# A fused attention and FFN kernel: final maxima moved to GpSimd, output tiles in halves, smaller last units split by head pair

## The chip, the cores and the metric

The kernel runs on one core of a Trainium2 chip. A core has five engines with queues of their own: TensorE (PE in the profile, its weight loads PEld), VectorE (DVE), ScalarE (ACT), GpSimd (POOL) and SyncE (SP), which here only issues DMAs. Matrix products land in PSUM, eight banks of 128 partitions x 512 fp32; everything else lives in SBUF. The metric is the device time of one execution in microseconds (us). Before the change it is 1213.11 us, the median of three runs (1212.67 to 1213.38).

## The reference

One layer with S = 2048 rows and D = 512 columns in bfloat16. `xn` is the layer norm of `x`. The result is `x + attention(xn) + ffn(xn)`:

```python
xn = _layernorm(x, axis=-1)
# attention: H = 32 heads of Dh = 16
qkv = (xn @ wqkv).reshape(B, S, 3, H, Dh).transpose(2, 0, 3, 1, 4)
q, k, v = qkv[0], qkv[1], qkv[2]
scores = jnp.einsum("bhqd,bhkd->bhqk", q, k) * (Dh ** -0.5)
p = _softmax(scores, axis=-1)
o = jnp.einsum("bhqk,bhkd->bhqd", p, v)
attn = o.transpose(0, 2, 1, 3).reshape(B, S, D) @ wo
# FFN: F = 1792
h = _silu(xn @ w1) * (xn @ w3)
out = x + attn + h @ w2
```

The softmax runs over 2048 keys for each of 32 x 2048 rows, so 134 million scores are computed, and their maximum per row is subtracted.

## The kernel before, in words

**Tiling.** Rows (queries) are cut into four chunks of 512 (`qc`), the 32 heads into eight groups of four (`g`). A pair (`qc`, `g`) is a head group; there are 32 of them, taken in order of `qc`, then `g`. Each is cut into *units* of 256 query rows; the first head group is cut 128, 128, 256 (`UNIT_HEAD`), and the last three into four units of 128 (`UNIT_TAIL`). That makes 71 units.

**First pass (p1).** For each unit the scores are computed with the queries on the partitions: one tile is 128 queries x 512 keys x two heads (a head pair), two matmuls in two row groups of PE (L878), into two PSUM banks. DVE reduces a tile to the maxima of its 128 rows for two heads (`part`, L900, 128x2 from 128x1024). There are 1024 such tiles, with two slots of two banks, so PE can write one tile while DVE reads the other. After a unit's last tile the maxima over the four key chunks are joined to `negm`, the negated row maximum (`final_max`, L941, on DVE). This instruction stands in DVE's queue behind one more tile of the next unit (`pend_fin`).

**The maximum enters the second scores as two more rows.** GpSimd splits `negm` in two bfloat16 numbers (L917 and L919, into `Z`). SP then transposes `Z` by DMA into `Zs` (L938) and copies two rows per head into the query tile `QT` (L934, two issues). For the units in `FAST_AUG` (the first two and the last four, `NFAST`) PE does this instead: the tile `QT2` projects the queries again from `xnT` (four groups of matmuls) and adds the transposed `Z` (one group for each 128 rows), and ACT copies it to `QT` (L696). For the last unit the two splitting steps are on DVE.

**Second pass (p2).** The scores are computed again with the keys on the partitions and the maximum already subtracted (L1014, one tile of 128 x 512, four of 256-column or 128-column matmuls by unit size), and ACT takes the exponential into `PT` (L1027, 2048 of them). Four PSUM banks serve p2 and all other products. A unit's tiles come for its four heads in turn.

**PV and the division.** `PT` times `V` with a column of ones gives 16 numbers and the sum for each head (`tile_PV`). ACT copies it to `U` (L1091); three small DMAs and GpSimd bring the reciprocal of the sums to all partitions (L1112, L1116, L1121, L1125), and GpSimd multiplies into `onorm` (L1136). For the units in `FAST_PV` (the last three, `NFPV`) PE also forms the sums over a block of ones, and DVE takes the reciprocal (L1081) and the product (L1083) from PSUM.

**FFN and output.** `ffn_pair` computes 128 columns of the hidden layer for 512 rows (two PE tiles, three copies on ACT, three steps on GpSimd, L720, L722, L724). An output tile of 128 rows (`tile_OUT`, 12 of them) is one accumulation over `x` (by the identity), 14 FFN groups and eight attention groups, copied by ACT (L802) and stored. The last four output tiles are in two passes: `tile_OUTA` holds `x` and the FFN part and is copied to SBUF by ACT (L818), `tile_OUTB` holds the eight attention groups, and DVE adds the two (L831).

**What sets the order.** The program is written out by a planner in Python (`_Prog` and the functions `pick_pe`, `pick_act`, `pick_dve`, `pick_pool`, `pick_sp`). It keeps a time at which each engine is free, with a cost for each instruction, and always emits what can start first; the order of each engine's queue is then fixed, with semaphore waits where a result is needed. On PE, row tiles (p1, p2) have due times (`late` in `pick_pe`): a p1 tile is due 0.7 us (`A_LEAD`) before DVE runs out of work, a p2 tile 0.55 us (`ROW_LEAD`) before ACT does. Column work (PV, FFN, output, projections) goes ahead of a row tile only if it ends by that due time (`TOL`). If little work was put on PE in the last 2.3 us (`low_load`), filler matmuls (`fill_cand`, xnT against the identity) are emitted. GpSimd's queue is fed from five lists, the splitting steps first, and takes the item that can start first.

## Time and profile before

| what | value |
|---|---|
| median of three runs | 1213.11 us |
| the profiled execution | 1211.87 us, span 1210.1 us |
| granted TensorE clock | 1.000 |
| DVE, first row maximum starts | 18.47 us |
| DVE, last row maximum ends | 1190.87 us |
| ACT, last exponential ends | 1204.52 us |
| POOL busy | 360.9 us |

The span is one profiled execution, from the first to the last instruction. Busy time counts an instruction from start to end; on DVE and ACT an instruction starts before the one ahead of it has ended, so distances between starts, from the timeline, say more than durations. In a timeline line the first number is the start in us, the second the length of the group, then engine, line, operation, output and input, and the count.

### The profile page before, as it was taken

To read this page: it belongs to the slowest core of one execution; us is meant where nothing else is said; L and a number is where in the kernel's file an instruction comes from. 1 tells how busy PE (TensorE), PEld (TensorE's weight loads), DVE (VectorE), ACT (ScalarE), POOL (GpSimd) and SP (SyncE) were. 2 spreads that over 40 slices of the span, in tenths; PEclk is the share of its full clock that TensorE was granted. 3 is DMA by queue.
4 is the path that set the end of the run, shared out by engine and by line. 5 is a ranking of instruction groups with operands and counts; after the bars stand their busy time and mean duration, and the time that the engine had idled before them with its cause. 6 is when DMAs were issued, how large, how long until landed. Compare 5 with 4: busy or idle time off the path is not lost.

```text
span 1210.1 us, 40652 instructions
## 1 busy us (share of the span) xinstructions
PE 1158.3 (96%) x17633; PEld 460.6 (38%) x17633; DVE 1191.3 (98%) x1154; ACT 1160.9 (96%) x2382; POOL 360.9 (30%) x470
## 2 busy tenths in 40 slices
PE   5999999999999999999999999999999999999998
PEld 2433333333333333333333333333333333334554
DVE  8999999999999999999999999999999999999995
ACT  5789999999999999999999999999999999999997
POOL 2234443635421135453111115553111111112210
PEclk9999999999999999999999999999999999999999
DMA  5422323222101022211001112211000111000000
GB/s 165 124 59 64 79 54 89 53 61 55 40 24 29 27 59 47 51 42 29 22 20 29 31 37 59 57 37 25 22 16 19 37 28 30 21 25 19 17 13 23
DMA packets 130303, 52.61 MB, mean 43 GB/s; under 512 B 99396, under 2 KB 130124, under 8 KB 130124
## 3 DMA queue, kind: packets, MB, share of 16 engines
q1 hardware_dynamic: 130124, 50.01, 16.4%
q8 instruction: 138, 2.26, 0.8%
q14 instruction: 41, 0.34, 0.1%
HBM read 38.73 MB, written 6.74 MB: 38 GB/s over the span
## 4 chain that ended last, share of the span: by engine, by line
ACT 49%; PE 33%; DVE 13%; issue 2%; POOL 1%; DMA 1%; SPq 0%; POOLq 0%
ACT PT L1027 42%; PE ps L491 18%; DVE part L900 13%; PE ps L1014 9%; PE ps L878 5%; ACT th L735 2%; ACT zg L737 2%; ACT U L1091 1%; ACT ub L741 1%; ACT kq L642 1%; PE ps L599 1%; ACT xnT L564 1%; DMA wk_on<-in_A_wqkv_dram 0%; POOL Rc L1116 0%; POOL hT L724 0%
## 5 line engine op out<-in xcount | busy, mean ns | idle before, releaser
L900 DVE TENSOR_REDUCE part<-ps 128x2 f32<-128x1024 f32 x1024 | 1167.8, 1214 | 1.8 <-PE ps L878 0.7
L1027 ACT ACTIVATE PT<-ps 128x512 bf16<-128x512 f32 x2048 | 1045.7, 650 | 6.1 <-PE ps L1014 5.0
L1014 PE MATMUL ps<-QT,KT 32*128 32x256 bf16 (+1 forms) x4544 | 566.9, 262 | 4.2 <-DVE wk_on L1083 0.3
L878 PE MATMUL ps<-KT,QT 32*128 32x512 bf16 x2048 | 437.6, 383 | 2.9 <-DVE part L900 2.3
L1014 PEld LDWEIGHTS ps<-QT,KT 32*128 32x128 bf16 x4544 | 215.7, 92 | 265.7 <-issue 108.0
L1116 POOL TENSOR_TENSOR Rc<-Lc,mone 128x8 f32<-128x8 f32 (+1 forms) x68 | 104.3, 1534 | 384.7 <-DMA Lc<-U 384.5
L491 PE MATMUL ps<-PT,Vaug 128*17 128x256 bf16 (+1 forms) x4544 | 191.0, 264 | 4.6 <-ACT zg L737 2.1
L491 PE MATMUL ps<-xnT,ident 128*32 128x512 bf16 x2048 | 162.0, 384 | 7.4 <-DVE part L900 0.5
L491 PE MATMUL ps<-xnT,w 128*32 128x512 bf16 x1792 | 149.0, 385 | 13.1 <-ACT zg L737 7.0
L878 PEld LDWEIGHTS ps<-KT,QT 32*128 32x128 bf16 x2048 | 113.6, 91 | 123.9 <-DVE part L900 56.4
L491 PEld LDWEIGHTS ps<-PT,Vaug 128*17 128x17 bf16 x4544 | 85.9, 89 | 100.6 <-issue 76.5
L722 POOL TENSOR_TENSOR a<-zg,ub 128x512 f32<-128x512 bf16 x56 | 64.6, 1153 | 61.8 <-ACT ub L741 61.6
L491 PE MATMUL ps<-w,hT 128*32 128x512 bf16 x896 | 79.7, 386 | 0.0
L724 POOL TENSOR_TENSOR hT<-a,t 128x512 bf16<-128x512 f32 x56 | 71.1, 1270 | 3.1
L491 PEld LDWEIGHTS ps<-xnT,w 128*32 128x32 bf16 x1792 | 39.3, 94 | 81.8 <-issue 72.1
L491 PEld LDWEIGHTS ps<-xnT,ident 128*32 128x32 bf16 x2048 | 40.1, 94 | 68.7 <-ACT PT L1027 50.1
L917 POOL TENSOR_SCALAR Z<-negm 128x8 bf16<-128x8 f32 (+1 forms) x70 | 15.7, 225 | 168.3 <-DVE negm L941 167.8
L1136 POOL TENSOR_TENSOR wk_on<-U,R 128x256 bf16<-128x256 f32 (+1 forms) x35 | 23.0, 658 | 105.2 <-DMA R<-rd 105.2
L1136 POOL TENSOR_TENSOR on_b<-U,R 128x256 bf16<-128x256 f32 (+1 forms) x33 | 23.4, 711 | 81.6 <-DMA R<-rd 81.5
L737 ACT ACTIVATE zg<-ps 128x512 bf16<-128x512 f32 x56 | 36.0, 643 | 0.0
L720 POOL TENSOR_SCALAR t<-th 128x512 f32<-128x512 bf16 x56 | 34.6, 618 | 4.6 <-ACT th L735 2.5
L741 ACT ACTIVATE ub<-ps 128x512 bf16<-128x512 f32 x56 | 35.7, 637 | 0.0
(78 smaller groups left out, 377.6 us busy)
## 6 DMA issues: line engine op xcount, KB each, us to landing
w<-in_B_w_dram SPq DMA_DIRECT2D x112, 128.0 KB
R<-rd SPq DMA_DIRECT2D x57, 128.0 KB
QT<-qd SPq DMA_DIRECT2D x31, 128.0 KB
KT<-kd SPq DMA_DIRECT2D x28, 128.0 KB
PT<-in_A_x_dram SPq DMA_DIRECT2D x4, 512.0 KB
xr<-in_A_x_dram SPq DMA_DIRECT2D x16, 128.0 KB
out_dram<-osb SPq DMA_DIRECT2D x16, 128.0 KB
qd<-kq SPq DMA_DIRECT2D x15, 128.0 KB
```

The lines of the kernel that those rows point to most:

```text
L491: ins = e.matmul(bank(bk)[32 * i:32 * i + m, c0:c0 + ncols], make_lhsT(i), rhs_ap(i), start=start, stop=stop, tile_position=(0, 32 * i), **kw)
L720: q.append(_Item(lambda e: e.tensor_scalar(t1[:, :], th[:, ss, :], 1.0, 1.0, ALU.mult, ALU.add), [("th", ss)], [("t1",)], 0.62, 0.72))
L722: q.append(_Item(lambda e: e.tensor_tensor(a32[:, :], zg[:, ss, :], ub[:, ss, :], ALU.mult), [("zg", ss), ("ub", ss)], [("a32",)], 1.1, 1.25))
L724: q.append(_Item(lambda e: e.tensor_tensor(hT[:, hslot(idx), :], a32[:, :], t1[:, :], ALU.mult), [("a32",), ("t1",)], [("hT", hslot(idx))] ...
L737: _Item(lambda e: e.activation(zg[:, ss, :], bank(bk), ACTF.Identity, scale=0.5), [("ps", bk)], [("zg", ss)], _c_act(512), cb=part_done, n ...
L741: return [_Item(lambda e: e.activation(ub[:, ss, :], bank(bk), ACTF.Identity), [("ps", bk)], [("ub", ss)], _c_act(512), cb=part_done)]
L878: ins = e.matmul(bank(2 * sl + i), QT[32 * j:32 * j + 32, qs, q * 128:(q + 1) * 128], KT[32 * j:32 * j + 32, g, kc * 512:(kc + 1) * 512], ...
L900: redq.append(_Item(lambda e: e.tensor_reduce(part[:, par, qt, 2 * pair:2 * pair + 2, kc], ps[:, sl * 1024:(sl + 1) * 1024].rearrange("p ( ...
L1014: ins = e.matmul(bank(b)[:, i * nq:(i + 1) * nq], KT[32 * j:32 * j + 32, g, (k0 + i) * 128:(k0 + i + 1) * 128], QT[32 * j:32 * j + 32, qs, ...
L1027: expq.append(_Item(lambda e: e.activation(PT[:, sl, :], bank(b), ACTF.Exp, scale=SCALE), [("ps", b)], [("PT", sl)], _c_act(512), cb=cb))
L1116: poolq["nrm"].append(_Item(lambda e: e.tensor_tensor(Rc[:, pp, 0:nl], Lc[:, pp, 0:nl], mone[:, 0:nl], ALU.pow), [("Lc", pp), ("mone",)], ...
L1136: poolq["nrm"].append(_Item(lambda e: e.tensor_tensor(onorm[ob][:, g, q0:q0 + nq], U[:, us, 0:nq], R[:, pp, 0:nq], ALU.mult), [("U", us)] ...
```

## The change

1. **Final maxima on GpSimd.** The row maxima L900 are now negated by the reduction itself (`negate=True`), so that joining them is a minimum. For the units in `FAST_AUG` that is one reduction on DVE, as before. For all others GpSimd does it in six steps: subtract, take the minimum with zero, add, for pairs of key chunks, and the same again. They go to GpSimd's first list, without the wait for one more tile.
2. **Smaller last units.** The last six head groups instead of the last three are cut into units of 128 rows (`NSMALL`), which makes 77 units. `NFAST` goes from 4 to 8, `NFPV` from 3 to 2.
3. **By head pair.** For the last four units (`NSPLIT`) the first pass takes all key chunks of one head pair and then of the other; each pair has its own final maximum, splitting steps and `QT2` tile, and its p2 tiles may start when its own `QT2` is there.
4. **QT2 by the identity.** The `QT2` tile takes the queries from `QT` by one group of matmuls with the identity, not by four groups from `xnT`. The padded weights `wq_last`, their memset and their copy go.
5. **Output in halves.** The 12 output tiles `tile_OUT` become 24 of 256 columns each, with the same groups.
6. **First pass of the last outputs.** `tile_OUTA` also takes five (`NG_A`) of the eight attention groups; `tile_OUTB` keeps three.
7. **The planner.** Column work may end up to 0.2 (`TOL_LOW`) after a row tile's due time if the recent load is under `LOAD_URG`; `low_load` also looks at half the window; one more bank may be let out while a `QT2` tile waits; the cost of the reciprocal is set to 0.87.

```diff
-    UNIT_TAIL = {1: (128, 128, 128, 128), 2: (128, 128, 128, 128), 3: (128, 128, 128, 128)}
-    NFAST = 4
-    NFPV = 3
+    TOL_LOW = 0.2
+    LOAD_URG = 9500
+    NG_A = 5
+    NSMALL = 6
+    UNIT_TAIL = {k: (128, 128, 128, 128) for k in range(1, NSMALL + 1)}
+    NFAST = 8
+    NFPV = 2
+    NSPLIT = 4
+    LOAD_HALF = 5000
...
+        NH_OUT = 2
...
-        def tile_QT2(u):
+        def tile_QT2(u, pairs):
...
-            groups = qt_groups(qc, g, q0, nq, False)
+            groups = [(lambda bk: mm(bk, lambda i: ident[:, 32 * i:32 * i + 32], QT[:, qs, q0:q0 + nq], nq, 0,
+                                     True, False),
...
-            groups = [g_x(tg)] + [g_h(tg, fc, fc == FC - 1) for fc in range(FC)]
+            groups = [g_x(tg)] + [g_h(tg, fc) for fc in range(FC)] + [g_on(qc, ts, g, False, g == NG_A - 1)
+                                                                      for g in range(NG_A)]
...
-            groups = [g_on(qc, ts, g, g == 0, g == NG - 1) for g in range(NG)]
+            groups = [g_on(qc, ts, g, g == NG_A, g == NG - 1) for g in range(NG_A, NG)]
...
             qc, g, q0, nq = units[u]
+            if u in SPLIT:
+                return [(u, 0, kc, pair) for pair in range(2) for kc in range(NQC)]
...
+                    if over:
+                        fin = final_max(u, pairs)
+                        if u == NU - 1 and p1_left[u] == 0:
                             redq.insert(0, fin)
+                        elif u not in FAST_AUG:
+                            poolq["z"] += fin
                         else:
                             pend_fin.append(fin)
...
-                    ps[:, sl * 1024:(sl + 1) * 1024].rearrange("p (a b) -> p a b", b=512), AX.X, ALU.max),
+                    ps[:, sl * 1024:(sl + 1) * 1024].rearrange("p (a b) -> p a b", b=512), AX.X, ALU.max,
+                    negate=True),
...
+            return [sub(d2, pv[:, :, 2:4], pv[:, :, 0:2], keys, ("fin_d",)),
+                    neg(d2, [("fin_d",)], ("fin_d",)),
+                    add(h2, d2, pv[:, :, 0:2], keys + [("fin_d",)], [("fin_h",)]),
+                    sub(d2[:, :, 0], h2[:, :, 1], h2[:, :, 0], [("fin_h",)], ("fin_d",)),
+                    neg(d2[:, :, 0], [("fin_d",)], ("fin_d",)),
+                    add(ng, d2[:, :, 0], h2[:, :, 0], [("fin_h",), ("fin_d",)], NK, cb=cb)]
...
+            if u in SPLIT:
+                p2_list.append([(kb, j) for p_ in range(2) for kb in range(NT // kpb) for j in (2 * p_, 2 * p_ + 1)])
...
-        outs += [tile_OUT(tg) for tg in range((NQC - 1) * 4)]
+        outs += [tile_OUT(tg, h) for tg in range((NQC - 1) * 4) for h in range(NH_OUT)]
...
+            most = (1 if red_n[0] < NP1 else 5) + (1 if crit and crit[0].need == -1 else 0)
...
-            if c[0] + c[2] <= late + TOL:
+            if c[0] + c[2] <= late + (TOL_LOW if load(P.free["pe"]) < LOAD_URG else TOL):
```

## The prediction

> **What bounds the kernel now.** I read the page first (its busy line), then the DVE's groups with their shapes, then the timeline, because "busy" hides pipelining, then the stretches near the end, and last the timeline of the end.
>
> The page:
> ```profile
> span 1210.1 us, 40652 instructions
> PE 1158.3 (96%) x17633; PEld 460.6 (38%) x17633; DVE 1191.3 (98%) x1154; ACT 1160.9 (96%) x2382; POOL 360.9 (30%) x470
> ```
> Three engines look full. They are not alike. In the timeline an exponential starts every 0.48 us when nothing holds it (32 of them took 15.36 us), so the 2048 exponentials need 983 us and ACT in all some 1110; its "1160.9" counts latencies that overlap. PE runs 511 filler groups (2048 matmuls of xnT against ident, 0.216 us a group, some 110 us) that do no work. DVE has neither reserve. Its groups, line, shapes, count, busy time and mean:
> ```profile
> L900 DVE TENSOR_REDUCE part<-ps 128x2 f32<-128x1024 f32 x1024 | 1167.8, 1214 | 1.8 <-PE ps L878 0.7
> L941 DVE TENSOR_REDUCE negm<-part 128x8 f32<-128x32 f32 x57 | 9.9, 173 | 0.0
> L941 DVE TENSOR_REDUCE negm<-part 128x4 f32<-128x16 f32 x14 | 2.2, 157 | 0.0
> ```
> The 1024 row maxima waited 1.8 us altogether. What a final maximum costs there shows only in the timeline (start, length):
> ```profile
> 972.45 0.17 DVE L941 TENSOR_REDUCE negm<-part 128x8 f32<-128x32 f32 x1
> 972.55 18.21 DVE L900 TENSOR_REDUCE part<-ps 128x2 f32<-128x1024 f32 x16
> 990.68 0.17 DVE L941 TENSOR_REDUCE negm<-part 128x8 f32<-128x32 f32 x1
> 990.77 18.18 DVE L900 TENSOR_REDUCE part<-ps 128x2 f32<-128x1024 f32 x16
> ```
> A lone maximum takes 1.21 us but the next starts 1.131 us after it; sixteen need 18.10 us. The next maximum starts 0.09 to 0.10 us after a final maximum's start: that, not 0.17, is what each costs DVE. From unit to unit (862.82 to 1008.96, eight units) it is 18.27 us, so 0.08 us a unit are small stalls, some 5 us over the run.
>
> Stretches at the end (PE, PEld, DVE, ACT, POOL busy, with counts), where units already have 128 rows:
> ```profile
> 1080.00:1110.00 30.00, 28.48 (x472) 11.57 (x468) 30.00 (x31) 28.50 (x60) 5.83 (x10) 1.00 0.07 16
> 1110.00:1140.00 30.00, 29.14 (x681) 16.20 (x678) 30.00 (x30) 30.00 (x65) 7.21 (x17) 1.00 0.09 19
> 1140.00:1170.00 30.00, 28.52 (x662) 15.49 (x654) 29.87 (x30) 28.96 (x63) 6.23 (x13) 1.00 0.07 14
> ```
> DVE stays full. Then the end:
> ```profile
> 1182.87 8.00 DVE L900 TENSOR_REDUCE part<-ps 128x2 f32<-128x1024 f32 x7
> 1190.91 0.17 DVE L941 TENSOR_REDUCE negm<-part 128x4 f32<-128x16 f32 x1
> 1193.66 0.27 ACT L696 ACTIVATE QT<-ps 128x128 bf16<-128x128 f32 x1
> 1198.83 1.57 ACT L1027 ACTIVATE PT<-ps 128x512 bf16<-128x512 f32 x3 [0.18 <-PE ps L1014]
> 1200.59 1.57 ACT L1027 ACTIVATE PT<-ps 128x512 bf16<-128x512 f32 x3 [0.19 <-PE ps L1014]
> 1202.35 2.17 ACT L1027 ACTIVATE PT<-ps 128x512 bf16<-128x512 f32 x4 [0.18 <-PE ps L1014]
> 1205.37 0.96 DVE L1081 RECIPROCAL R<-ps 128x128 f32<-128x128 f32 x1 [3.06 <-PE ps L491]
> 1207.16 0.69 DVE L831 TENSOR_TENSOR osb<-ps,zg 128x512 bf16<-128x512 f32 x1 [0.51 <-PE ps L491]
> ```
> So the span is: head, then the DVE stream until 1190.87, then 19.2 us of tail, 13.65 of it until the last exponential (1204.52) and 5.54 for reciprocal, product, last output group, sum and store.
>
> **The change, part by part.**
>
> *Final maxima off DVE.* Units go from 71 to 77. The two units at the start and the last eight keep DVE; the last four of these have two finals each: 2+4+8 = 14 on DVE against 71. Before the last row maximum 57 fewer stand there, all in effect of the 128x32 form. 57 x 0.095 = 5.4 us off the stream; ends 57 x 0.09 = 5.1 and 57 x 0.17 = 9.7 if the whole instruction went. The spacing measures it, so 5.4.
>
> *Negation.* All 1024 maxima are now negated; none of that size is in the trace. Bound: the negated small forms take 157 ns for 16 inputs and 173 for 32, 1.0 ns an input; from the 32-input form to 1214 ns at 1024 it is 1.05 ns an input. The unnegated row lies on the negated line to about 10 ns, so zero, with ±10 ns (±10 us in all) as ends; I keep zero since a fixed charge would have shown in the 173.
>
> *The six GpSimd steps.* 67 units x 6 = 402 instructions, nearest row L917/L919, 0.23 us, 0.3 us start to start when each waits for the one before. That is some 120 us on an engine busy 361 of 1210: hidden there. Their latency is not free: from a unit's last maximum to the second Z step it was 1.13 (the final stands behind one more maximum) + 0.57 = 1.7 us; now about 0.1 + 7 x 0.3 = 2.2. Behind this stand the transposing DMA (1.2 us issue), two row DMAs on SP and then the unit's first score matmul L1014, which sits in PE's queue ahead of later L878 matmuls. A late Z would thus stop PE, and after it DVE. The cover: in the order of the queues the first score matmul of a unit stands 7 to 28 maxima after the unit's last L878; in the tightest units (7 to 9 maxima) it started 2.2 to 3.9 us after the second row DMA's issue. In the changed order the tight units stand at 8 to 10 up to the last ten units, mostly one maximum (1.13 us) further back, which covers the 0.5 us. In FFN stages GpSimd's FFN steps (0.62, 1.15, 1.27 us) and some waits for DMAs come between the six; there the distance is 10 to 26 maxima. Cost 0; if the cover failed, see the rivals.
>
> *Small units.* Twelve more units of 256 rows become 24 of 128. Maxima, exponentials and matmul columns are the same. ACT: 13 more U copies of 128 (0.16 us: 1179.77 to the next start 1179.93), 6 fewer of 256 (0.26), 8 more QT copies (0.16), 24 half output copies for 12 whole (24 x 0.26 - 12 x 0.48): +2.3 us against 100 spare. SP: 27 more issues net; a small unit takes 3.8 us of its queue (transposing issue 1.2, two row issues 1.07, three for the sums 0.57, 0.32 and 0.60) of 9.1, as it already does from 1110 on. PE: the stretches above: the matmul count rises from 472 to 681 in 30 us, weight loading from 11.6 to 16.2 us, and DVE is still at 30.00. Twelve score matmuls of 128 columns took 0.44 us, four 0.39: some 10 to 20 ns each, because four row groups work side by side. Cost 0.
> [...]
>
> *Output tiles in halves, QT2 by identity.* A group of 128 columns takes 0.055 us and one of 512 0.216, so halves cost PE nothing; the QT2 tile falls from five groups to two. The cleared 0.27 us memset of wq_last lay before a wait for x (DVE idle 2.52 until 4.83): nothing.
>
> *Fill rule and tolerance.* With little recent load, column work may start 0.2 us past the due time of a row matmul. In the trace a maximum starts 0.04 to 0.6 us after its L878 matmuls end, median 0.31, a tenth under 0.08. Ends: 0, and a mean of 0.1 us on the quarter with under 0.2 us, 1024 x 0.27 x 0.1 = 28 us, if it applied everywhere. In the order, PE's work between two L878 pairs has the same spread (95% at 0.8 us of 1.131 before and after; over 1.0 in 6 and 4 cases), so I take 0, near the lower end.
>
> *The tail.* After the last L878 25 score tiles (100 matmuls) follow before, 22 after, because the last unit's first head pair is started four maxima earlier; output groups after it fall from 32 to 12, since five of eight are in the first pass, where they replace filler. Three tiles fewer: 3 x 0.48 = 1.45 us. Between 1198.83 and 1202.35 three exponentials took 1.76 us instead of 1.44, as six output groups (1.48 us) stood in between, three times: 0.95 us, gone. Sum 2.4; the 5.54 at the end stays. Upper end: 25 x 0.48 + 0.16 = 12.2 us were needed from the last L878 (1188.8) to 1204.52, 15.7 were taken, so at most 1.45 + 3.5 = 4.9. Lower end: unit 74, third from last, is now normalised by GpSimd and DMAs, and PE waits for it in the tail. That path took 8.1 us (U copy at 1179.77, product done 1187.88). By the order some 15 exponentials must be done after that copy before PE gets to the wait, and up to four more tiles are then issued and keep ACT busy: 19 x 0.48 + 0.3 = 9.4 us, 1.3 us of cover. If it is 3 us short beyond that, the tail gains nothing: -0.6.
>
> Sum: 5.4 + 2.4 = 7.8 us off the profiled execution's 1211.87 (span 1210.1 + 1.8 around it), so 1204.1, span 1202.3. The median of the runs shown is 1.2 above the profiled run: 1213.1 - 7.8 = 1205.3.
>
> **The rivals.**
> 1. *The tail gives nothing* (unit 74 late, or ACT stays behind: 18 exponentials still follow the last QT copy, against 19). Only 5.4: 1207.7, with a microsecond or two of added stalls up to 1210. Chance 0.15.
> 2. *GpSimd's chain stops PE* (the other side). Place: first score matmul of the tight units, some 22. Price: Z is 0.5 us later by steps, plus up to 1.64 us (Rc, the 0.23 us step behind it at 973.47) where it slips in. From 7.8/22 = 0.35 us per tight unit on, all is lost; at 0.8 us each 17.6 - 7.8: 1223. For it: the p2 margin of 2.2 us after issue is nearly the landing itself. Against: the order stands back by one maximum. Chance 0.08.
> 3. *PE bound in the small units.* If the extra weight loading (4.6 us in 30) were not hidden over 12 x 9.05 = 109 us: +16.7, so 1222. Against: 30.00 and 29.87. Chance 0.02. [...]
> 4. *The tolerance or the negation costs DVE* 6 to 10 ns a maximum: 6 to 10 us, 1211 to 1216. Chance 0.07.
>
> **How the numbers follow.** Forecast 0.68 (1202.5 to 1207.5), rivals 0.15, 0.08, 0.02, 0.07. A measurement tells about 0.2%, 2.4 us. Faster: forecast and rival 1, 0.83. Same (1210.7 to 1215.5): most of rival 4 and a mild rival 2, 0.06. Slower 0.11. The range goes from 1202 (tail's upper end, stalls unchanged) to 1211 (rival 1 and the mild part of 4).
>
> **What would show it.** Right: DVE's group of finals at 14, the big maxima still 1214 ns and 1.131 apart, their last end near 1185.5, a tail of about 16.8 us with fewer "PE ps" waits before the last exponentials. Wrong: DVE idle before maxima well above 1.8 us, released by the matmuls L878 wrote; PE waiting for POOL's Z; a big maximum above 1220 ns; PE waiting for POOL in the last 12 us.

## The result and the profile after

| | median us | profiled execution | last maximum ends | tail behind it |
|---|---|---|---|---|
| before | 1212.91 (1212.67 to 1213.38) | 1211.87, span 1210.1 | 1190.9 | 19.2 |
| after | 1224.94 (1220.48 to 1225.71) | 1224.54, span 1222.7 | 1204.1 | 18.6 |

The ratio is 1.0091, 95% interval 1.0067 to 1.0116: slower by 11 to 12 us where I had forecast 7.8 us less. That is under 1%, but the four executions after (1220.48 the lowest) all lie above the four before. All of it lies in the stream of row maxima, which ends 13.2 us later. The tail (span less the last maximum's end) is 0.6 us shorter.

The first lines of the page of after, with the clock's row of its 40 slices:

```profile
span 1222.7 us, 44357 instructions
...
PE 1172.5 (96%) x19281; PEld 506.5 (41%) x19281; DVE 1188.3 (97%) x1094; ACT 1167.8 (96%) x2409; POOL 457.4 (37%) x905
...
PEclk9999999999999999999999999999999999689998
```

The shares are those of before. The granted clock is not: it was 1.000 in the profile of before and 0.983 here, and the digits 6 and 8 say where. DVE's groups of after (line, tile, shapes, count, busy time and mean, idle time ahead and what ended it):

```profile
L941 DVE TENSOR_REDUCE part<-ps 128x2 f32<-128x1024 f32 x1024 | 1167.0, 1223 | 15.9 <-PE ps L1088 11.4 <-PE ps L912 2.8
...
L995 DVE TENSOR_REDUCE negm<-part 128x2 f32<-128x8 f32 (+1 forms) x14 | 2.2, 157 | 0.0
```

The finals on DVE are down to 14, as the change says, and the distance of two maxima is still 1.131 us (median). But the maxima now waited 15.9 us, 14.2 of it for PE; before it was 1.8 and 0.7. Summed over the stream, what the distances have above 1.131 us is 27.3 us against 14.2. The finals' part fell from 6.8 to 2.1, and the rest, stalls, rose from 7.3 to 25.2.

The stretches of the last 200 us of after (length; busy time of PE, weight loading, DVE, ACT, GpSimd with counts; granted clock; DMA):

```profile
1020.00:1050.00 30.00, 28.33 (x590) 16.86 (x582) 24.56 (x22) 24.88 (x53) 9.89 (x31) 0.80 0.11 27
1050.00:1080.00 30.00, 28.50 (x602) 15.86 (x600) 26.85 (x23) 26.23 (x54) 8.96 (x28) 0.84 0.13 30
1080.00:1110.00 30.00, 29.12 (x576) 14.86 (x570) 28.42 (x25) 26.67 (x56) 8.79 (x28) 0.91 0.09 22
...
1170.00:1200.00 30.00, 28.06 (x561) 15.15 (x558) 27.61 (x31) 28.39 (x64) 7.82 (x22) 0.91 0.06 12
1200.00:1230.00 30.00, 17.95 (x444) 10.27 (x436) 8.91 (x14) 13.76 (x28) 1.45 (x2) 0.81 0.07 21
```

DVE is short where the clock is (in the last line it has also run out of maxima, from 1204.1 on). The clock records have two values only, 1.0 and 0.5, in stretches that are multiples of 3.41 us: half clock from 1037.7 to 1058.2, 1078.7 to 1085.5, 1187.9 to 1191.3 and 1198.1 to 1208.4, 41 us together. The first of them, before and during it:

```profile
1034.00:1037.70 3.70, 2.07 (x48) 1.27 (x40) 2.02 (x2) 1.94 (x6) 1.83 (x9) 1.00 0.02 5
1037.70:1058.20 20.50, 20.50 (x344) 11.02 (x340) 14.67 (x12) 14.80 (x29) 4.06 (x11) 0.50 0.10 24
```

In these 20.50 us at half clock PE counts as busy without a gap, and DVE has only 14.67 us of work. What stood ahead of it is in the timeline (start, length, engine, line, tile, and in brackets the wait), here for GpSimd, SP's queue, PE and DVE one after the other:

```profile
1023.59 0.20 POOL L999 TENSOR_TENSOR fin_d<-part 128x8 f32<-128x8 f32 x1 [2.97 <-DVE part L941]
1025.69 0.46 POOL L1210 TENSOR_TENSOR wk_on<-U,R 128x128 bf16<-128x128 f32 x1 [1.91 <-DMA R<-rd]
1026.12 0.25 POOL L1005 TENSOR_SCALAR fin_d<-fin_d 128x8 f32<-128x8 f32 x1
...
1027.63 0.21 POOL L970 TENSOR_SCALAR Z<-negm 128x4 bf16<-128x4 f32 x1
1027.78 1.03 POOL L1190 TENSOR_TENSOR Rc<-Lc,mone 128x4 f32<-128x4 f32 x1
1028.78 0.22 POOL L972 TENSOR_TENSOR Z<-negm,Z 128x4 bf16<-128x4 f32 x1
...
1029.21 1.13 SPq L991 DMA_TRANSPOSE Zs<-Z  x1
1030.38 0.57 SPq L1199 DMA_DIRECT2D R<-rd  x1
1033.98 1.09 SPq L987 DMA_DIRECT2D QT<-Zs  x2
...
1036.24 0.38 PE L1088 MATMUL ps<-QT,KT 32*128 32x128 bf16 x4 [1.63 <-DMA QT<-Zs]
...
1037.80 1.23 DVE L941 TENSOR_REDUCE part<-ps 128x2 f32<-128x1024 f32 x1 [1.78 <-PE ps L1088]
```

The unit's last maximum ended at 1023.5, and a chain of steps leads from there to the first score matmul. Between the first of GpSimd's six new steps and the second stands a product (L1210) that waited 1.91 us for a DMA, and between the two Z steps a 1.03 us step (L1190): the second Z step started 5.3 us after the maximum, where I had estimated 2.2. The transposing DMA issued at 1029.21 let the row DMAs go at 1033.98 only, 4.8 us later; the planner counts 2.3. So PE waited 1.63 us, and had little work in that stretch of 3.41 us. Half clock follows right behind; whether the wait as such brings it or the little work is what the runs below ask.

### The profile page after: what moved, and what is told of

Read it like the earlier page. It is cut to its first block, busy times and chain, and to the rows that moved or that the text cites. A ratio compares the mean times of both kernels' runs of the same rounds, so it can differ in the third digit from the quotient of the medians.

```text
span 1222.7 us, 44357 instructions
## 1 busy us (share of the span) xinstructions
PE 1172.5 (96%) x19281; PEld 506.5 (41%) x19281; DVE 1188.3 (97%) x1094; ACT 1167.8 (96%) x2409; POOL 457.4 (37%) x905
## 3 DMA queue, kind: packets, MB, share of 16 engines
q1 hardware_dynamic: 132564, 49.94, 16.5%
## 4 chain that ended last, share of the span: by engine, by line
ACT 51%; PE 32%; DVE 7%; DMA 6%; POOL 2%; issue 2%; SPq 0%; ACTq 0%; POOLq 0%
ACT PT L1101 44%; PE ps L498 16%; PE ps L1088 9%; DVE part L941 7%; PE ps L912 5%; ACT th L755 2%; DMA R<-rd 2%; ACT zg L757 1%; DMA rd<-Rc 1%; PE ps L606 1%; DMA Zs<-Z 1%; POOL Rc L1190 1%; ACT U L1165 1%; ACT kq L649 1%; ACT ub L761 1%
## 5 line engine op out<-in xcount | busy, mean ns | idle before, releaser
L941 DVE TENSOR_REDUCE part<-ps 128x2 f32<-128x1024 f32 x1024 | 1167.0, 1223 | 15.9 <-PE ps L1088 11.4
L1088 PE MATMUL ps<-QT,KT 32*128 32x256 bf16 (+1 forms) x4928 | 579.5, 257 | 5.7 <-DMA QT<-Zs 2.6
L1088 PEld LDWEIGHTS ps<-QT,KT 32*128 32x128 bf16 x4928 | 235.9, 94 | 238.6 <-issue 104.8
L1190 POOL TENSOR_TENSOR Rc<-Lc,mone 128x8 f32<-128x8 f32 (+1 forms) x75 | 109.1, 1455 | 245.4 <-DMA Lc<-U 245.3
L498 PEld LDWEIGHTS ps<-PT,Vaug 128*17 128x17 bf16 x4928 | 90.7, 90 | 93.3 <-issue 63.8
L498 PE MATMUL ps<-w,hT 128*32 128x256 bf16 (+1 forms) x1568 | 84.2, 297 | 0.0
L999 POOL TENSOR_TENSOR fin_d<-part 128x16 f32<-128x16 f32 (+1 forms) x67 | 14.0, 210 | 165.1 <-DVE part L941 164.9
L1210 POOL TENSOR_TENSOR wk_on<-U,R 128x128 bf16<-128x128 f32 (+1 forms) x42 | 24.5, 584 | 125.0 <-DMA R<-rd 125.0
L1210 POOL TENSOR_TENSOR on_b<-U,R 128x256 bf16<-128x256 f32 (+1 forms) x33 | 23.4, 710 | 87.5 <-DMA R<-rd 87.5
L498 PEld LDWEIGHTS ps<-w,hT 128*32 128x32 bf16 x1568 | 34.0, 96 | 32.5 <-issue 26.6
L1005 POOL TENSOR_SCALAR fin_d<-fin_d 128x8 f32<-128x8 f32 (+2 forms) x134 | 34.8, 260 | 9.7
```

What stands on the lines that cost most here:

```text
L498: ins = e.matmul(bank(bk)[32 * i:32 * i + m, c0:c0 + ncols], make_lhsT(i), rhs_ap(i), start=start, stop=stop, tile_position=(0, 32 * i), **kw)
L941: redq.append(_Item(lambda e: e.tensor_reduce(part[:, par, qt, 2 * pair:2 * pair + 2, kc], ps[:, sl * 1024:(sl + 1) * 1024].rearrange("p ( ...
L1005: return _Item(lambda e: e.tensor_scalar(o, o, 0.0, 0.0, ALU.min, ALU.add), r, [w], 0.25)
L1088: ins = e.matmul(bank(b)[:, i * nq:(i + 1) * nq], KT[32 * j:32 * j + 32, g, (k0 + i) * 128:(k0 + i + 1) * 128], QT[32 * j:32 * j + 32, qs, ...
L1190: poolq["nrm"].append(_Item(lambda e: e.tensor_tensor(Rc[:, pp, 0:nl], Lc[:, pp, 0:nl], mone[:, 0:nl], ALU.pow), [("Lc", pp), ("mone",)], ...
L1210: poolq["nrm"].append(_Item(lambda e: e.tensor_tensor(onorm[ob][:, g, q0:q0 + nq], U[:, us, 0:nq], R[:, pp, 0:nq], ALU.mult), [("U", us)] ...
```

## The experiments

All are compared with the kernel before, run beside them (median 1212.3 to 1212.8). "After" means the changed kernel. "Lag" is the number of row maxima begun minus half the exponentials begun, at a given time: how far the second pass is behind the first.

**Is it the finals' place?** The finals of after back on DVE:

```diff
-                        elif u not in FAST_AUG:
-                            poolq["z"] += fin
-            if u in FAST_AUG:
+            if True:
                 return _Item(lambda e: e.tensor_reduce(ng, pv, AX.X, ALU.min), keys, NK, 0.093, 0.262, cb=cb)
```

> The changed kernel with every final maximum back on DVE, one reduction each, behind one more row maximum as before; all else changed. Theory A (GpSimd's chain makes Z late, PE waits for the rows at the tight units, the clock halves and DVE starves): the PE waits on QT<-Zs go, the granted clock is back at 0.99 or more, and the time is 1213 less the tail (2.4) plus ten more finals than before (0.9): 1211 to 1213. Theory B (the small units themselves bring PE down, whoever makes the maxima): the clock still falls below 0.99 and the time is 1224 plus 6 us of finals, about 1230.

Measured 1222.8 (1216.1 to 1230.6), ratio 1.0099 [1.0066, 1.0132]. Neither: the harm stays without GpSimd's six steps. PE still waited 2.6 us for rows, three times, as in after. The half clock around 1037 to 1085 is absent from its profile, but there is some at 725.9 to 729.3, 1176.4 to 1183.2 and 1196.9 to 1207.1. Its executions follow their mean clock: 1216.1 at 1.000, 1222 at 0.990, 1230 at 0.982.

**The finals on GpSimd alone**, put into the kernel before (the six steps, negated maxima, nothing else):

> The kernel before with the first part alone: negated row maxima, final maxima in six GpSimd steps for all but the first two and last four units; units, outputs and planner rules as before. In its order the first score matmul of a unit stands 16 to 35 maxima behind the unit's last one. Theory A: with that distance nothing waits for Z, the row maxima keep 1.131 us, and the time falls by the 57 finals, 5.4 us, to about 1207.5, clock 1.00. A rival (the negation, or GpSimd's extra steps, cost DVE something of their own): 1213 or more, with row maxima longer than 1.131 apart.

Measured 1220.9 (1218.6 to 1223.6), ratio 1.0072 [1.0056, 1.0088], at a clock of 0.993 to 0.998. The stream of maxima ended 3.4 us earlier (1187.5), but the tail was 32.4 us, not 19.2. So a shorter stream on DVE alone bought nothing: something else was later. Both forecasts miss that; the distance of two maxima is still 1.131 us, so the rival named there is not it.

**GpSimd's queue alone**: in after, a unit's eight steps put side by side in GpSimd's queue; all other queues as they are.

```diff
+    def chains_together(self):
...
+            if open_ and not o.name.startswith("fin"):
+                late.append(o)
+                continue
...
         P.check()
+        P.chains_together()
```

> The changed kernel with GpSimd's queue alone reordered: what stood between a unit's eight steps (six for the maximum, two for Z) now stands behind them; every other queue is the same. Theory A in its narrow form (the steps are late because other GpSimd work and its waits stand between them): Z starts 2.2 to 2.6 us after the last maximum everywhere, against up to 9.2, and the time is 1205 to 1212. If the row DMAs' own lateness is enough (after the transposing DMA's issue 2.8 to 6.5 us pass before the rows are issued), PE still waits at some units in the small stage, the clock still falls there and the time stays at 1215 to 1225.

Measured 1214.8 (1211.2 to 1222.4), ratio 1.0023 [1.0001, 1.0044]. The second Z step now starts 2.28 us after the unit's last maximum (median), 4.14 at worst; in after 3.06 and 9.24. The time lies between the two forecasts. Some 8 us (1.0091 to 1.0023) go with the order of one engine that is busy 37% of the time. Its ten executions go from 1211 at a clock of 0.995 to 1222 at 0.984; the profiled one is of the latter, with half clock at 127.5 to 148.0, 1182.3 to 1189.1 and 1195.9 to 1206.2, and 1.5 us of waits for rows. So the lateness is less, but not gone.

**The planner's price of the transposing DMA alone**: 4.5 us for 2.3 in after.

```diff
-                    ZK, [("Zs", par)], cb=rows_dma, occ=1.25)
+                    ZK, [("Zs", par)], cb=rows_dma, occ=1.25, lat=4.5)
```

> The changed kernel with one number of the planner changed: it takes 4.5 us for the transposing DMA instead of 2.3, so that it puts the first score matmul of a unit one to two maxima later (10 to 12 at the tight units); no work changes. Theory A: PE finds the rows there, the clock stays at 0.99 or more and the time is 1204 to 1209. Theory B: the small stage still loses the clock, 1218 to 1226.

Measured 1216.1 (1214.5 to 1218.6), ratio 1.0035 [1.0022, 1.0048]. Again neither forecast. PE no longer waited for rows at all, yet the profile has half clock at 1072.3 to 1075.8 and 1174.7 to 1195.2. Late rows are one cause among others.

**One wait put into the kernel before**: the same price at 0.6 us for one unit.

```diff
-                    [("Z", par)], [("Zs", par)], cb=rows_dma, occ=1.25)
+                    [("Z", par)], [("Zs", par)], cb=rows_dma, occ=1.25, lat=0.6 if u == 64 else 2.3)
```

> The kernel before with one fault put in: for unit 64 alone the order is planned as if the transposing DMA took 0.6 instead of 2.3 us, so that PE reaches that unit's second pass before its rows have landed. All work is the same. Theory A (a wait of PE lets the granted clock fall, and PE at half clock can't feed DVE, for at least one more window of 3.41 us): the profile shows one wait of PE of 1 to 2 us on a rows' DMA (QT<-Zs) around unit 64, half clock for 3.4 to 20 us right behind it, and a time 3 to 10 us above the kernel before: 1215 to 1223. Theory B (a PE wait costs at most itself, and DVE's queue of waiting scores takes most of it up): the same wait, clock 1.00 throughout, 1212.4 to 1214.

Measured 1212.97, ratio 1.0005 [0.9995, 1.0014]. Inconclusive: the wait that came of it was 0.3 us long, so the question was not put.

**The tail's parts alone**: finals on DVE as above, and `NSMALL = 3`.

> The changed kernel with the final maxima back on DVE and with three small units in the last column group instead of six: what is left is the split of the last four units by head pair, eight units on the fast path, the halves of the output tiles, the five groups in the first pass and the new rules for fill and tolerance. Theory A (the drops of the clock in the last 30 us come from the units split by head pair, the earlier ones from the small-unit stage): no drop before 1150, one behind 1175, 1213 to 1217. Theory B (the tail's parts do what I had forecast of them, and the harm is in GpSimd's finals and small units): 1208 to 1211, clock 1.00 to the end.

Measured 1230.0 (1225.4 to 1236.1), ratio 1.0147 [1.0111, 1.0183], worse than both theories. Its stretches around the first drop:

```profile
1162.90:1166.30 3.40, 3.40 (x76) 2.20 (x74) 3.40 (x5) 3.40 (x9) 0.95 (x1) 1.00 0.02 1
1166.30:1176.50 10.20, 10.20 (x168) 6.35 (x161) 7.32 (x8) 7.94 (x18) 2.21 (x7) 0.50 0.05 10
```

By the busy figure PE had no gap at all in the 3.40 us before the clock fell. That figure counts a 128-column matmul for some 0.22 us (median 219 ns in before), though in a row those of L558 there start 0.056 us apart (median), so it hides short pauses; but the longest time without a new matmul was 0.23 us. What was low was the work: the matmuls that began there stream 10624 columns (40 of 128 for PV, 27 of 128 for the second pass, four of 512 for the first). So here the clock fell with no long wait ahead of it. That asked for a count over all traces. (The clock isn't all that this run loses: its fastest execution, at 0.998, still took 1225.4. The runs with three small units below come back to that.)

**The count.** In after the eight changes of the clock listed above lie whole multiples of 3.413 us apart. With a grid of such steps laid through the clock records of each of the 20 profiles of this case, without the first 30 us and the last 10 or so, I added up the columns that the matmuls beginning in a step stream (128, 256 or 512 each), and noted the clock in the next step. The bounds are rough: a few per cent of the matmul records can be missing, and a grid set 0.05 us to one side moves each count by up to five.

| clock in the step | columns | steps | half clock in the next |
|---|---|---|---|
| 1.0 | under 11300 | 18 | 18 |
| 1.0 | 11300 to 13000 | 84 | 7 |
| 1.0 | 13000 and more | 6679 | 0 |
| 0.5 | under 11000 | 72 | 70 |
| 0.5 | 11000 to 12000 | 17 | 11 |
| 0.5 | 12000 and more | 17 | 0 |

In after, some 5600, 11800, 10200 and 9900 columns stood ahead of the four drops. The lower half of the table is what makes a drop expensive: 72 of the 106 steps at half clock stream fewer than 11000 columns, and 70 of these were followed by another. The grid also stands at another place relative to the program in after than in before (a step begins 0.07 us past a multiple of 3.413 us from the span's start in one, 1.96 us in the other), so a thin stretch may be cut in two by it in one execution and not in the next. That would explain why one kernel gives 1209 in one execution and 1219 in the next, as the following one does.

**No split by head pair**: `NSPLIT = 0` in after, all else kept.

> The changed kernel with no unit split by head pair (all else as in the change, finals on GpSimd and six small units included). Theory A: the drop of the clock in 1015 to 1085 stays, since it comes from the late chain of GpSimd in the small units, and the drops in 1175 to 1208 go: 1217 to 1222. Theory B (the split doesn't matter, the last units are short of PE work either way): both drops stay, 1223 to 1226.

Measured 1216.3 (1209.4 to 1219.1), ratio 1.0021 [1.0003, 1.0039]. By execution: 1209.4 at clock 0.999, 1211.8 to 1212.1 at 0.995 to 0.996, 1215.6 to 1219.1 at 0.986 to 0.992. That is just under theory A's band. The profiled one is the first, with no drop before the end. Up to 1169 us its queues hold the same work in the same order as those of after, so the two profiles can be compared there. The transposing DMA that let its row DMAs wait 4.8 us in after let them go after 2.2 here, and PE didn't wait at 1036. It did wait later, 1.07 us at 1051.6 and 0.81 at 1062.3. Around these waits there are stretches of 3.41 us with only some 7400 columns (begun at 1048.5) or 7600 columns (begun between 1058.5 and 1060.5), and yet the clock held: the grid cut each of them in two, and its own steps there hold 12500 to 16500. So in these two profiles the clock went with the work in a step of the grid, not with that in any 3.41 us. What happened at 1020 to 1085 in the slower executions isn't seen.

**More filler**, a test of the table: two bounds of the planner, in after. The work that counts stays the same, but the planner also writes a somewhat different order for it (ACT's queue differs from 40 us on).

```diff
-    LOAD_MIN = 14500
+    LOAD_MIN = 17500
-    LOAD_HALF = 5000
+    LOAD_HALF = 7500
```

> The changed kernel with more filler matmuls and nothing else: the planner's bounds for a low PE load go from 14500 and 5000 to 17500 and 7500, which makes 524 fillers of 482 (each four 128x512 matmuls whose product nobody reads). Theory A (the time is lost because single 3.41 us stretches of PE work are too thin for the clock to hold): useless work makes the kernel faster, 1212 to 1219, with fewer us at half clock than the 41 of the changed kernel's profile. Theory B (PE is short of time, or the clock falls because of the waits themselves): same or slower, 1224 to 1230.

Measured 1212.4 (1209.7 to 1220.9), ratio 1.0012 [0.9990, 1.0033]. 42 more groups of matmuls that nobody reads take 10 to 12 us off the changed kernel (by ratio and by median); half of its executions are at 1209.7 to 1210.5, with a clock of 0.997 to 0.999, the others at 1214 to 1221 with 0.984 to 0.995. In the profile, one of the fast ones, the stretch that lost most in after (0.80 there) has 3.4 us at half clock left:

```profile
1020.00:1050.00 30.00, 29.70 (x735) 19.30 (x734) 29.72 (x27) 29.33 (x63) 11.00 (x32) 0.94 0.12 28
```

Theory A: PE was not short of time; it was short of work. With the table and the executions that follow their clock, this is what the stream of maxima was lost to. As the order changed too, it doesn't show that the filler did it all by itself.

**Three repairs together**: order of GpSimd's steps, 4.5 us, no split.

> The changed kernel with three things together: GpSimd's eight steps of a unit stand together in its queue, the order is planned with 4.5 us for the transposing DMA, and no unit is split by head pair. Theory A (drops of the clock are all that the change loses, and these are their causes): no PE wait above 1 us, clock at least 0.997, stream of maxima about 5 us shorter than in the kernel before, 1205 to 1210. Theory B (with the clock whole, ACT and the second pass still hold the end back, as in the run with the finals alone): stream shorter but tail longer, 1211 to 1216.

Measured 1208.4 (1207.7 to 1210.9), ratio 0.9972 [0.9959, 0.9984]: faster than both kernels (by 0.3% and 1.2%), and theory A; no PE wait for rows is left. Clock 0.996 to 1.000. The profile has DVE's row back where it was before the change, and the stream's end 4.1 us earlier than there:

```profile
L969 DVE TENSOR_REDUCE part<-ps 128x2 f32<-128x1024 f32 x1024 | 1164.1, 1214 | 1.8 <-PE ps L940 0.8
...
1178.77 8.00 DVE L969 TENSOR_REDUCE part<-ps 128x2 f32<-128x1024 f32 x7
1186.81 0.17 DVE L1023 TENSOR_REDUCE negm<-part 128x4 f32<-128x16 f32 x1
```

The span ends at 1206.2, a tail of 19.4 us: what is left of the tail's parts gave nothing.

**The same with the split**:

> The changed kernel with GpSimd's eight steps of a unit together in its queue and the order planned with 4.5 us for the transposing DMA, with the last four units still split by head pair (the run that also took the split out gave 1208.4). Theory A (the split by head pair is a cause of its own for the thin PE work of the last 40 us): half clock for 3.4 to 20 us between 1155 and 1205 in most executions, 1212 to 1217. Theory B (with the chain in order the split does no harm): 1207 to 1210, clock at least 0.997.

Measured 1218.1 (1210.7 to 1220.0), ratio 1.0034 [1.0020, 1.0049]: theory A, a microsecond worse: half clock in the profile from 1171.6 to 1195.5, one execution without a drop at 1210.7. So the two repairs together are no better than either alone (ratios 1.0034 against 1.0023 and 1.0035), and with the runs above they make a table of two by two: after 1.0091, the chain repaired 1.0023 to 1.0035, the split taken out 1.0021, both 0.9972. By these ratios the late chain costs some 6 to 8 us and the split some 7 to 9, both by the clock, and the two add up. Where the clock holds, the split brings nothing either: the tail is 19.1 us in the profile of the run with more filler, where the units are split, and 19.4 in the 1208.4 run. Why its units stream fewer columns isn't settled.

**What the finals are worth with the clock held**: 4.5 us and no split, finals on DVE.

> The run that gave 1208.4 with its 57 final maxima back on DVE and the queue of GpSimd as it comes: six small units, output halves, five groups in the first pass, 4.5 us for the transposing DMA, no split. It measures what GpSimd's finals are worth once the clock holds. Theory A (the 5.4 us that I forecast for the finals arrive when the clock holds): 5 us more, 1212 to 1215. Theory B (ACT and the second pass hold the end, DVE's finals cost nothing): 1207 to 1210. A result between is a share of the 5.4.

Measured 1215.0 (1214.1 to 1226.7), ratio 1.0032 [1.0012, 1.0052]. Against 1208.4 that is 6.6 us for 67 finals (77 on DVE here and 10 there; the 57 of the text above was the difference to the kernel before), and the stream ends 6.8 us later (1193.6); 67 x 0.095 = 6.4. So theory A: the forecast's price of a final is right.

**And in the kernel before, with the first two repairs and the finals on GpSimd**:

> The kernel before with the final maxima on GpSimd, as in the run that gave 1220.9, but with GpSimd's eight steps of a unit together and the order planned with 4.5 us for the transposing DMA; the tail's parts, halves and small units are those of before. Theory A (GpSimd's finals are worth 5.4 us less what the late rows cost, and these two repairs take that cost away): 1207 to 1210, clock at least 0.997, tail near 20 us. Theory B (ACT and the second pass are the second bound, so that a shorter stream of maxima only gives a longer tail): 1211 to 1214 with a stream of maxima that ends 3 to 5 us earlier and a tail of 23 us or more.

Measured 1222.7 (1221.8 to 1224.0), ratio 1.0085 [1.0069, 1.0100], at a clock of 0.995 to 0.998: still 10 us slower, so late rows aren't what made the finals alone a loss. The stream ends at 1188.0, the tail is 32.9 us, the lag at 1150 us is 28.5 (before: 15.5, best run: 16.5). Theory B has the direction, but not the size, which it put 9 us lower. Of the 12.5 us that 13 more maxima of lag are worth in exponentials (13 x 2 x 0.48), 7.3 us can be seen as ACT's longer waits for output tiles. Before, then this run (us in total, times, longest); the 1208.4 run has no such line:

```profile
ACT osb L802 <- PE ps L491: 12.2, 9, 2.1
```

```profile
ACT osb L832 <- PE ps L521: 19.5, 11, 3.2
```

The planner fixes the order of ACT's queue. An eviction of a whole output tile that ACT reaches before PE has finished its 23 groups holds all exponentials behind it, here 11 times and for up to 3.2 us. The middle of the run, the kernel before, this kernel and then the 1208.4 run:

```profile
638.00:838.00 200.00, 193.74 (x2786) 73.92 (x2782) 199.72 (x187) 196.78 (x404) 71.71 (x86) 1.00 0.16 40
838.00:1038.00 200.00, 196.20 (x2802) 71.86 (x2798) 199.89 (x187) 192.91 (x395) 32.44 (x46) 1.00 0.10 26
```

```profile
638.00:838.00 200.00, 195.09 (x2704) 73.85 (x2696) 199.69 (x177) 192.59 (x397) 82.18 (x147) 1.00 0.16 39
838.00:1038.00 200.00, 196.77 (x2828) 74.22 (x2826) 199.88 (x177) 194.11 (x400) 53.29 (x117) 1.00 0.10 25
```

```profile
638.00:838.00 200.00, 195.83 (x3156) 80.88 (x3148) 199.25 (x176) 197.77 (x409) 76.73 (x141) 1.00 0.16 39
838.00:1038.00 200.00, 195.53 (x3564) 88.99 (x3560) 199.81 (x177) 198.31 (x413) 66.80 (x159) 1.00 0.10 27
```

ACT (fourth busy time) is busy 386.7 us of these 400 here and 396.1 in the 1208.4 run; before it was 389.7. DVE is full in all three. With DVE faster, ACT is the engine that falls behind.

**Whole output tiles in the 1208.4 run**:

```diff
-        NH_OUT = 2
+        NH_OUT = 1
-                note_load(st, 1024 if t.name.startswith("PV") or t.paced else 2048)
+                note_load(st, 1024 if t.name.startswith("PV") else 2048)
```

> The run that gave 1208.4 (finals on GpSimd, eight steps together, 4.5 us for the transposing DMA, no split) with whole output tiles instead of halves: one eviction of 128x512 on ACT for each tile and 28 matmul groups of 512 columns ahead of it. Theory A (ACT is the second bound, and it is the halves that keep it from waiting for output tiles, so that the finals' gain shows only with them): ACT waits some 15 to 20 us for output tiles (none with the halves), the second pass is over 20 maxima behind when the maxima end, tail 28 us or more, 1216 to 1223. Theory B (the halves cost nothing and bring nothing): 1207 to 1210, tail near 20.

Measured 1229.5 (1227.6 to 1238.9), ratio 1.0156 [1.0110, 1.0203]. ACT's wait for output tiles is back, the lag at 838 us is 47.5 (33.0 with halves), and the tail is 30.8 us:

```profile
ACT osb L857 <- PE ps L526: 16.0, 10, 2.5
```

(A whole tile has 23 groups, not the 28 of the text above.) The profile also has 34 us at half clock from 1116 on. The executions go from 1227.6 at a mean clock of 0.989 to 1238.9 at 0.975; carried on to 0.999 that would be some 1220, an estimate, inside theory A's band. So the excess over the band is put down to the clock; that is argued, not shown.

**More filler in the 1208.4 run**:

> The run that gave 1208.4 with the raised bounds for filler (17500 and 7500). Theory A (thin stretches are all gone already, the filler only takes PE time): 1208 to 1211, nothing gained, and no execution below clock 0.997. Theory B (the executions of the other run that fell to 0.996 to 0.998 still lost something): 1206.5 to 1208, spread under 1.5 us.

Measured 1209.3 (1208.1 to 1212.8), ratio 0.9978 [0.9969, 0.9988]. Theory A, nothing gained: there the clock is no longer what costs (one execution did fall to 0.994).

**Three small units in the 1208.4 run** (`NSMALL = 3`, `NFAST = 4`, `NFPV = 3`):

> The run that gave 1208.4 with three small units, four units on the fast path and three on the fast PV path, as in the kernel before. Theory A (the six small units bring nothing to the tail and cost six more finals and thin PE work): 1206 to 1208.5. Theory B (they shorten the tail by the 2.4 us that I gave the tail's parts together, or hold the clock better than large units without a split): 1210 to 1213, with a tail of 21 to 24 us.

Measured 1234.6 (1225.9 to 1240.3), ratio 1.0174 [1.0129, 1.0219]. Neither theory: I had expected no harm. The lag doesn't fall: 26.5 at 1150 us, against 16.5. In the order that the planner writes out, the last outputs' first pass stands at maxima 947 to 1011 of 1024 here, at 933 to 993 in the 1208.4 run, and at 863 to 903 before: with five attention groups in it, it must wait for the second pass to get that far. So I took the groups out:

```diff
-    NG_A = 5
+    NG_A = 0
-            groups = [g_x(tg)] + [g_h(tg, fc) for fc in range(FC)] + [g_on(qc, ts, g, False, g == NG_A - 1)
+            groups = [g_x(tg)] + [g_h(tg, fc, stop=fc == FC - 1) for fc in range(FC)] + [g_on(qc, ts, g, False, g == NG_A - 1)
```

> The run with three small units that gave 1234.6, with the last outputs' first pass as in the kernel before: no attention groups in it, so that it need not wait for them. In the order it then stands at maxima 881 to 919 of 1024, not 947 to 1011. Theory A (the five groups make the first pass wait for the second pass, so that its 80 wide matmul groups come into the last units, where PE has to feed the exponentials; this is what costs with three small units): ACT keeps up, the second pass is under 18 maxima behind at 1150 us (25 in the run with the groups), 1208 to 1214. Theory B (large units at the end are themselves the cause, by their size): the lag stays above 22, 1225 or more.

Measured 1211.5 (1211.1 to 1215.1), ratio 0.9996 [0.9986, 1.0005]; lag 19.0 at 1150 us, ACT busy 146.4 us of the 150 from 1038 on (135.7 with the groups). Theory A holds in the time, and nearly in the lag, which it put under 18: the groups in the first pass cost 23 us there, the clock's part included (13.6 us at half in the profile with them, none before the end without).

> The run that gave 1208.4 (six small units) with no attention groups in the last outputs' first pass. Theory A (the five groups were harmless there, since the first pass is over by maximum 993, and save matmuls behind the last exponential): 1208 to 1211, the tail 1 to 3 us longer. Theory B (the late first pass costs there too): 1205 to 1207.

With six small units they cost and bring nothing: 1208.5 (1207.8 to 1209.8), ratio 0.9969 [0.9956, 0.9982], which is theory A but for the tail (19.0). Six small units, with the eight units on the fast path and two on the fast PV path that come with them, are worth 3 us against three (1211.5 to 1208.5).

> The run with whole output tiles that gave 1229.5, with no attention groups in the last outputs' first pass: in the order the first pass then stands at maxima 885 to 963, not 943 to 1024. Theory A (whole tiles alone make ACT wait for output tiles and keep the second pass 40 maxima behind, whatever the first pass does): 1216 to 1223, the same as the finals on GpSimd in the kernel before. Theory B (the whole tiles harmed by pushing the first pass into the last units): 1207 to 1212.

Measured 1244.3 (1241.7 to 1257.2), ratio 1.0282 [1.0228, 1.0337]. Theory B falls: whole tiles do harm without the late first pass (ACT waits the same 16.0 us, lag 48.0 at 838 us). Theory A's size is far off, and its profile, of the slowest execution, shows the clock again, 126 us at half:

```profile
1038.00:1188.00 150.00, 149.14 (x2348) 77.51 (x2344) 117.80 (x104) 121.62 (x241) 37.09 (x109) 0.64 0.07 16
```

PE counts as busy for 149 of 150 us and keeps neither DVE nor ACT full. Which stretch began it, and why more than in the run with whole tiles above, stays open.

## Why the prediction was wrong, by its steps

The step that failed most is one that the working doesn't have. I put the six GpSimd steps and the small units at cost 0 and the split at a gain. I asked whether PE would wait or be short of time, and gave the granted clock, 1.000 before, no term at all. What the runs showed in its place: PE's work got thin in single steps of 3.41 us, the clock was at half for 41 us of the profile, and the stalls of DVE's stream rose from 7.3 to 25.2 us. The parts that brought it about are GpSimd's late chain (6 to 8 us) and the split (7 to 9 us); the ratios above show that. How each of them thins PE's work is shown for the late rows alone.

- **Finals off DVE, 5.4 us: size right, condition missed.** 0.095 us each; 67 finals gave 6.6 us once the clock held and the output tiles were halved. In the kernel before they gave a loss of 8 to 10 us with or without the repairs. The condition is the "100 spare" that I gave ACT. That sum over the whole run was no reserve, since ACT loses time to waits in the fixed order of its queue: in the kernel before it was busy 389.7 us of the 400 from 638 to 1038, with DVE at 399.6.
- **Negation, 0: right.** 1.131 us from maximum to maximum; mean 1214 ns again in the 1208.4 run. The mean isn't a good sign of trouble, though: over the negated runs it goes from 1214 to 1224 ns, 1222 in the one at 1208.5, and the distance stays.
- **The six GpSimd steps, cost 0: wrong.** The estimate of 2.2 us from maximum to second Z step held for steps that follow one another (2.28 median when put side by side). The order let other steps, with waits for DMAs, between them: 3.06 median, 9.24 worst. I had seen such steps, but put them only where the distance was 10 to 26 maxima. Rival 2 named the place and even the time (1223), but that is luck: its price was 22 waits of 0.8 us on PE, and PE waited for late rows and Z 3.5 us in all, four times. The rest was the clock. Nor are the steps alone to blame: with the finals back on DVE the rows were late as often.
- **Small units, cost 0: half right.** PE was not bound by their count, so rival 3 fell: of the 25.2 us of stalls, 13.5 touch stretches at half clock, and in the 1208.4 run, with as many small units, all stalls come to 9.3. They bring 3 us. But their stage has thin stretches, and I read only PE's busy time, which was 28 to 29 of 30 us and said nothing of that. One count was wrong: six units of 256 rows become twelve, not twelve 24 (71 units become 77). The costs that I added up have the right counts.
- **Halves, cost 0: not 0, but a gain.** They keep ACT from waiting; without them the best version loses 21 us, the clock's part included. That they turn the finals into a gain is argued from the pairs of runs above; halves in the kernel before, with nothing else, weren't run.
- **Fill rule and tolerance, 0.** The tolerance wasn't tried by itself, so its cost stays open; the filler is the lever that I passed over. I wrote that the first passes "replace filler" as if filler were worthless. (There are 512 groups of it before, by the row's 2048 matmuls, not 511.)
- **The tail, 2.4 us: wrong, rival 1 was right about it.** 19.2 before, 18.6 after, 19.4 in the 1208.4 run; which of rival 1's two reasons held wasn't looked into. The split brought nothing where the clock held, and 7 to 9 us of loss where it didn't. The five groups changed nothing with six small units and cost 23 us with three.

Together: with the clock held, the change without its split and with the chain repaired is worth 4 us (1208.4), not 7.8: finals 6.6, and 2.3 lost by the rest (the run with the finals on DVE is at 1215.0; its stalls are 9.8 us, 2.5 more than before). As it was written, thin PE work cost it the clock for 41 us and the stream of maxima 18 us of stalls.

## What to carry to other kernels

Here busy time of PE didn't tell whether its clock would hold (28.33 us of 30 in a stretch at 0.80, 28.48 of 30 before in one at 1.00); the matmul columns in each 3.41 us step did, as far as the count goes. So add them up, and treat filler as a resource with a due place, not as waste: 42 more groups of it took 10 to 12 us off. When the bounding engine is relieved, look at the next one's waits in its own queue before counting the gain; here, as far as these runs go, halving an eviction on ACT decided the sign of a change on DVE. And parts of a change that wait for one another (first pass on second pass, rows on GpSimd's queue) have to be priced together, since each alone may be a loss.

## What the runs showed of the hardware

In these traces the clock fell after one thin step of 3.41 us (18 of 18 under 11300 columns, none of 6679 from 13000 on). Ahead of one drop PE had no long gap: 10624 columns, with 3.40 us of 3.40 counted as busy. No PE wait near the four drops of after was above 1.63 us. The clock came back after each of the 17 steps at half clock with 12000 columns or more; of the 89 with fewer, 81 were followed by another one, in stretches of up to 20.5 us in after and 88.8 us in the last run. A stretch as thin that two steps share was followed by no drop (7400 columns in the run without the split, at a clock of 1.0).

So here the work in the step told of a drop, and the longest wait didn't: PE waited 1.07 us at 1051.6 in the run without the split, and the clock held; with 3.40 us of 3.40 counted as busy it fell.

The first row DMA of a unit was issued 4.8 us after the transposing DMA in the case shown, where 2.57 was the median of after and 2.73 of before (5.9 and 4.2 the longest, the wait for SP's turn included). For the same unit it was 2.2 us in the run without the split. So in these traces it is a latency with a tail, and the fixed order, priced at 2.3 us, didn't hold the long end of it.
